# Idle products, two low halves and an early GpSimd call in a memory-attention mixer

## The chip, the cores and the metric

The kernel runs on one core of one Trainium2 chip. The metric is the device time of one execution in microseconds (us); lower is better. The engines are named as in the profile: PE (TensorE matmul), PEld (TensorE weight load), DVE (VectorE), ACT (ScalarE), POOL (GpSimd), SP (SyncE, which issues the DMAs).

## The reference, cut to what matters

Eight batches, eight heads, 576 positions, head dimension 64, 32 memory slots. First an attention over a memory, then a token and channel mixer:

```python
a = softmax(phi, axis=slots)                       # phi [8, 8, 576, 32]
k_m, v_m = einsum('bhsm,bhsd->bhmd', a, k), einsum('bhsm,bhsd->bhmd', a, v)
attn = softmax(q @ k_m.T / sqrt(64), axis=slots) @ v_m
x = attn as [8, 576, 512]
h = maximum(x.T @ w_tok1, 0) @ w_tok2              # 576 -> 256 -> 576
u = x + h.T
out = u + maximum(u @ w_ch1, 0) @ w_ch2            # 512 -> 1536 -> 512
```

The weights come as 64-bit words. The kernel turns them on the chip into a high and a low fp32r part each; a product with full precision is then three matmuls (high by high, high by low, low by high).

## The kernel before, in words

The batches are cut into 9 chunks of 512 columns for the channel mixer, and each batch into two quads of four heads (quad `(b, Q)`, tile names end in the quad). A quad runs: softmax of phi, `kvp` (or `kp` and `vp` apart in the first batch), keys turned (`Tp`, `kb`), scores `sp`, softmax `S`, the attention `aT` and its high and low parts, `Ap` and `Rp` (the token mixer), `u`. Then the chunk's channel mixer takes `uh` and `ul`: products `cp` (with `c1h`, `c1l`), their relu parts `hh` (ACT) and `hl` (DVE), products `acc` (with `c2`).

Two stages have their order set in different ways. The **front** is batches 0 and 1, the conversion of the weights and the first chunk. A planner (`plan`) with a cost and a set of buffers for every step draws up one order for all engines; the code is then written out in that order, so each engine's queue is fixed. From the second chunk on a **table of slots** (`at`, `run`) sets the order: two slots for each of a chunk's 12 products of `cp`, with steps of the next quads put at slots (`k` is the place within a slot). Instructions wait by semaphores for their inputs and for free buffers; each engine works through its queue strictly in that order.

Places that the change touches:

- **Idle products.** `ps_tile` puts `fill` matmuls of the identity by itself into a PSUM bank just before a step of the front takes that bank. They compute nothing that is read. `fill` is worked out from the planned gap of PE before the step.
- **The early GpSimd call.** Right after the constants a `partition_all_reduce` runs on a scratch tile on POOL (L104). Its result is not used. In POOL's program a library index is reloaded wherever the queue passes from plain operations (such as `TENSOR_TENSOR`) to `PARTITION_ALL_REDUCE` or back: ahead of L104, ahead of the first weight low part `w1l` (L644), and later ahead of the first `phi_max` of the slot table (L261).
- **The third batch's first quad, (2, 0)** (class `ThirdBatchQuad`, held in `second`). `a_pair` writes the high half of the attention on ACT and subtracts it on POOL for the low half (L455, L456), two pairs.
- **The next quad, (2, 1)**: `phi_max` (DVE, then POOL), `phi_exp` (subtraction on DVE, exponential on ACT), `phi_sum` (DVE, then POOL), placed at slots `m - 7`, `m - 4` and `m - 3`.

In the front two more names matter. `raww` tiles are the raw words of the token weights, turned by ACT (L610, L622, L626), DVE (L616, L633) and then split by ACT (L640) and POOL or DVE (L644). Quad (0, 1) keeps its scores in the tile `k`, whose keys are used up by `kp` before; POOL clears its tail (L1113) ahead of the exponential (L414).

Of the kernel before, what the change touches and what calls it, by code (L numbers as in the profile page):

```python
# [15 lines left out]
ALU = mybir.AluOpType  # L16
AX = mybir.AxisListType
PSUM = bass.MemoryType.PSUM
RED = bass_isa.ReduceOp

P = 128
# [7 lines left out]
def kernel(  # L29
# [25 lines left out]
    nc = tc.nc  # L55
# [36 lines left out]
    for a in range(2):  # L92
# [3 lines left out]
    small = [  # L96
        wp.tile([P, n], F32, tag=tag, name="small" + tag, bufs=bufs)
        for tag, n, bufs in (("mx", 4 * NC, 2), ("ms", 6, 1))
    ]
# [1 line left out]
        nc.gpsimd.memset(t, 0.0)  # L101
    warm = wp.tile([P, 1], F32, tag="ps", name="warm", bufs=2)
    nc.scalar.activation(out=warm, in_=small[1][:, :1], func=AF.Exp)
    nc.gpsimd.partition_all_reduce(small[0][:, :6], small[1], P, RED.max)  # L104


    w1h = wp.tile([P, NC, TT], F32R, name="w1h")
# [7 lines left out]
    def f32(t):  # L115
        return t.bitcast(F32)
# [16 lines left out]
    def wide(dtype, name):  # L133

        return sb.tile([P, NKK, CW], dtype, tag="wide", name=name, bufs=5)


    class Chunk:
        def __init__(s, c):
            s.c, s.n, s.hid = c, f"_{c}", {}  # L140
            s.uh = wide(F32R, "uh" + s.n)
            s.ul = wide(F32R, "ul" + s.n)
# [79 lines left out]
    def mixer(c):  # L222
        if c not in chunks:
            chunks[c] = Chunk(c)
        return chunks[c]
# [2 lines left out]


    class Quad:  # L230
        def __init__(s, b, Q):
            s.b, s.Q, s.n = b, Q, f"_{b}_{Q}"

# [217 lines left out]
        def a_pair(s, p):  # L451

            own, other = slice(64 * p, 64 * p + 64), slice(64 - 64 * p, P - 64 * p)
            h, l = s.pairs[p][own], s.pairs[p][other]
            nc.scalar.copy(out=h, in_=s.aT[own])  # L455
            nc.gpsimd.tensor_tensor(out=l, in0=s.aT[own], in1=f32(h), op=ALU.subtract)  # L456

        def v_pairs(s):

# [303 lines left out]
    def step(eng, us, fn, *after, take=(), use=(), move=0.0, port=False, other=None):  # L763
        steps.append(Step(eng, us, fn, after, list(take), list(use), move, port, other))
        return steps[-1]
# [630 lines left out]
    class ThirdBatchQuad(SecondQuad):  # L1396


        attend = Quad.attend

        def step_kv(s):
            s.kvp = bank([P, CW], "kvp" + s.n)
# [131 lines left out]
    for Q, h0 in ((0, 3), (1, 11)):  # L1534
        qd = quads[1, Q]
        late = 4 if not Q else 0
# [11 lines left out]
    z = second.plan_phi()  # L1548
    step("SP", 0.62, second.load_kv, take=[kv2], move=3.5)
    step("SP", 0.62, second.load_q, quads[1, 1].x_s, take=[q2], move=1.6)  # L1550
    o0, y = Room(("wide", 5)), products[-4]
    for x in range(NKK):
        y = step(
            "POOL", 1.4, lambda x=x: chunks[0].residual([x]), *a.lows, *c.lows, y,
            use=[*room0] + ([o0] if x else []), take=[] if x else [o0],
        )
# [7 lines left out]
    for z in order:  # L1564
        if z.eng == "PE":
            if z is products[0]:
                break
            gap = z.begin - max(idle, 2.0)
            if gap > 1.0 and z.take:
                z.fill = int(0.42 * gap / 0.24)  # L1570
            idle = z.end
    for z in order:
        now[0] = z
# [6 lines left out]
    def at(h, fn, *x, k=0):  # L1580
        events.setdefault((max(h, 0), k), []).append((fn, x))

    beside = {}
    for b in range(2, B):
        for Q in range(2):
            qd = second if b == 2 and not Q else Quad(b, Q)
            r = 2 * NF * b - (14 if Q else 26)
            if b == 2 and not Q:
                r = m = 2 * NF
            else:  # L1590

                m = r - (0 if b == 2 else 10 if b > 3 or Q else 8)
                at(max(m - 11, 2 * NF), qd.load_phi)
                at(m - (6 if (b, Q) == (3, 0) else 7), qd.phi_max, k=1)
                at(m - 4, qd.phi_exp, k=1)
                at(m - 3, qd.phi_sum, k=1)
                at(loaded + 1, qd.load_kv, k=1)
                at(r - 4, qd.load_q, k=1)
            loaded = m
            at(m, qd.step_kv)  # L1600
            at(m + 4, qd.values)
            if b > 2:
                at(m + 3, qd.get_keys, k=1)
            else:
                at(m + 1, qd.step_T)
            at(r + 2, qd.step_s)
            if Q or b == 2:
                at(r + 3, qd.sm2)
            else:
                beside[r + 3] = qd  # L1610
            at(r + (3 if qd is second else 4), qd.a_pair, 1)
            at(r + 6, qd.nat, k=1)
            at(r + 7, qd.v_pairs)
            at(r + 8, qd.step_A)
            at(r + 9, qd.step_R)
            for x in range(4):
                at(r + 10 + x // 2 * (1 if qd is second else 2), qd.step_u, x // 2, x % 2)
        at(2 * NF * (b - 1) + 7, lambda b=b: mixer(b).take(), k=1)
    for c in range(CHUNKS):
        h = 2 * NF * (c + 1)  # L1620
# [5 lines left out]
        if h + 1 in beside:  # L1626
            qd = beside.pop(h + 1)
# [125 lines left out]
```

## Time and profile before

| what | value |
|---|---|
| median of 3 runs | 780.65 us (780.28 to 783.66) |
| the profiled execution, its own time | 776.89 us |
| its span, first to last instruction | 775.1 us |
| mean granted TensorE clock of it | 0.993 of full speed |
| PE busy | 763.0 us, 98% of the span |
| DVE, ACT, POOL busy | 363.1, 249.6, 136.1 us |

The profile is of one execution, which took 776.89 us, of which 1.79 us lie around the span; the three timed runs took 3.4 to 6.8 us longer than it. Times inside the trace count from the start of the span. A PE that is busy is not always doing work that the result needs: idle products count as busy.

### The profile page before, as it was taken

The numbers are of one execution on the slowest core, as the hardware profiler recorded it, in microseconds if no ns is written. First come the engines' busy times: TensorE is split into PE (matmuls) and PEld (weight loads), VectorE is DVE, ScalarE is ACT, GpSimd is POOL, SyncE is SP. The second block draws the span as 40 slices with busy tenths as digits, with TensorE's granted clock in tenths as the row PEclk, the third lists the DMA queues.
The fourth block names the chain that finished last, engine by engine and source line by source line (L and its number), as shares of the span: only waits on it lengthen the run. The fifth ranks groups of instructions, "written<-read, shape, count | busy, mean of one in ns | idle before, by whom it ended". The sixth has DMA issues, their size and how long they took to land.

```text
span 775.1 us, 11131 instructions
## 1 busy us (share of the span) xinstructions
PE 763.0 (98%) x4520; PEld 633.9 (82%) x4520; DVE 363.1 (47%) x617; ACT 249.6 (32%) x481; POOL 136.1 (18%) x118
## 2 busy tenths in 40 slices
PE   7999999999999999999999999999999999999998
PEld 6777888777878888887878887888888888888887
DVE  4978874646454443635354445444352512212114
ACT  5789664232314232323223231423232311110110
POOL 1234223112211013101320121101310402002000
PEclk8999999999999999999999999999999999999999
DMA  9945420332406040514024130604040101001001
GB/s 322 417 152 206 172 99 9 89 114 84 136 3 204 1 151 2 145 60 122 30 37 169 19 134 5 203 1 150 2 120 1 32 1 54 1 1 54 1 1 54
DMA packets 52674, 68.93 MB, mean 89 GB/s; under 512 B 33680, under 2 KB 42896, under 8 KB 48400
## 3 DMA queue, kind: packets, MB, share of 16 engines
q1 hardware_dynamic: 52048, 67.71, 26.3%
q8 instruction: 35, 0.57, 0.3%
q10 hardware_dynamic: 576, 0.52, 0.2%
q14 instruction: 15, 0.12, 0.1%
HBM read 54.92 MB, written 13.30 MB: 88 GB/s over the span
## 4 chain that ended last, share of the span: by engine, by line
PE 83%; DVE 7%; issue 5%; DMA 3%; POOL 1%; ACT 1%; SPq 0%; DVEq 0%; ACTq 0%; POOLq 0%
PE cp L159 34%; PE acc L192 32%; PE u L549 7%; PE Ap L509 3%; PE u L1203 2%; DMA k<-in_kv_dram 1%; PE Rp L528 1%; DMA rawc<-in_w_ch_dram 1%; DVE o L210 1%; PE end L192 1%; PE kvp L296 1%; PE sp L392 1%; DVE S L423 1%; DVE S L399 1%; DVE mx L406 0%
## 5 line engine op out<-in xcount | busy, mean ns | idle before, releaser
L192 PE MATMUL acc<-hh,c 128*128 128x512 f32 x832 | 277.7, 394 | 0.8
L129 DVE SCALAR_TENSOR_TENSOR hl<-cp,hh 128x512 fp32r<-128x512 f32 x104 | 71.7, 689 | 271.7 <-ACT hh L126 271.7
L192 PEld LDWEIGHTS acc<-hh,c 128*128 128x128 f32 x832 | 156.2, 188 | 39.9 <-issue 6.1
L159 PE MATMUL cp<-uh,c1h 128*128 128x512 f32 x432 | 163.4, 392 | 0.0
L159 PE MATMUL cp<-ul,c1h 128*128 128x512 f32 x432 | 162.5, 390 | 0.0
L192 PE MATMUL acc<-hl,c 128*128 128x512 f32 x416 | 162.4, 390 | 0.0
L159 PE MATMUL cp<-uh,c1l 128*128 128x512 f32 x432 | 162.3, 389 | 0.0
L126 ACT ACTIVATE hh<-cp 128x512 fp32r<-128x512 f32 x104 | 61.9, 596 | 268.7 <-PE cp L159 268.7
L159 PEld LDWEIGHTS cp<-uh,c1l 128*128 128x128 f32 x432 | 81.1, 188 | 17.0
L159 PEld LDWEIGHTS cp<-ul,c1h 128*128 128x128 f32 x432 | 81.2, 188 | 16.6
L159 PEld LDWEIGHTS cp<-uh,c1h 128*128 128x128 f32 x432 | 80.6, 188 | 17.1 <-issue 1.1
L192 PEld LDWEIGHTS acc<-hl,c 128*128 128x128 f32 x416 | 78.2, 188 | 13.9
L456 POOL TENSOR_TENSOR a<-aT,a 64x576 fp32r<-64x576 f32 x24 | 34.3, 1430 | 202.2 <-ACT a L455 116.6
L204 POOL TENSOR_TENSOR o<-uh,ul 128x512 f32<-128x512 f32 x36 | 48.7, 1380 | 116.5 <-PE cp L159 46.9
L250 DVE TENSOR_REDUCE pr<-phi 128x128 f32<-128x640 f32 x22 | 29.0, 1319 | 12.5 <-ACT phi L274 8.1
L455 ACT CAST a<-aT 64x576 fp32r<-64x576 f32 x24 | 16.2, 673 | 56.0 <-DVE aT L429 55.7
L549 PE MATMUL u<-w2l,Rh 128*128 128x288 f32 x112 | 33.1, 295 | 0.0
L549 PE MATMUL u<-w2h,Rh 128*128 128x288 f32 x112 | 33.0, 295 | 0.0
L549 PE MATMUL u<-w2h,Rl 128*128 128x288 f32 x112 | 32.9, 294 | 0.0
L574 DVE TENSOR_TENSOR ul<-u,uh 128x288 fp32r<-128x288 f32 (+8 forms) x48 | 17.1, 356 | 21.8 <-ACT uh L568 21.5
L129 DVE SCALAR_TENSOR_TENSOR Rl<-Rp,Rh 128x512 fp32r<-128x512 f32 x14 | 9.6, 687 | 35.9 <-ACT Rh L126 35.9
L283 POOL PARTITION_ALL_REDUCE psr<-pr x11 | 11.9, 1081 | 70.3 <-issue 48.9
(199 smaller groups left out, 883.7 us busy)
## 6 DMA issues: line engine op xcount, KB each, us to landing
kv<-in_kv_dram SPq DMA_DIRECT2D x12, 1280.0 KB, 6.8
rawc<-in_w_ch_dram SPq DMA_DIRECT2D x12, 1024.0 KB, 7.6
q<-in_q_dram SPq DMA_DIRECT2D x16, 576.0 KB, 5.9
out_dram<-o SPq DMA_DIRECT2D x8, 1024.0 KB, 7.4
phi<-in_phi_dram SPq DMA_DIRECT2D x16, 320.0 KB, 4.0
kv<-in_kv_dram SPq DMA_DIRECT2D x6, 640.0 KB, 10.5
rows<-S SPq DMA_DIRECT2D x48, 72.0 KB, 2.0
raw<-rows SPq DMA_DIRECT2D x12, 256.0 KB, 2.8
```

Source lines behind the costliest of these rows:

```text
L126: nc.scalar.activation(out=h, in_=ps, func=AF.Relu)
L129: nc.vector.scalar_tensor_tensor(out=l, in0=ps, scalar=0.0, in1=f32(h), op0=ALU.max, op1=ALU.subtract)
L159: nc.tensor.matmul(ps, l[:, a, w], r[:, a], start=n == 0, stop=n == len(mm) - 1)
L192: nc.tensor.matmul(ps, l_[f // 2][:, f % 2, a * P : (a + 1) * P], r[:, w], start=f == start and x == 0, stop=f == end - 1 and x == 2,)
L204: nc.gpsimd.tensor_tensor(out=s.o[:, a], in0=f32(s.uh[:, a]), in1=f32(s.ul[:, a]), op=ALU.add)
L250: nc.vector.tensor_reduce(out=m.rearrange("p (i m) -> p i m", i=4), in_=s.pt.rearrange("p i j m -> p i m j"), axis=AX.X, op=op,)
L455: nc.scalar.copy(out=h, in_=s.aT[own])
L456: nc.gpsimd.tensor_tensor(out=l, in0=s.aT[own], in1=f32(h), op=ALU.subtract)
L509: nc.tensor.matmul(ps[:, :TT], a, w, start=x == 0, stop=x == len(mm) - 1)
L549: nc.tensor.matmul(ps[:, :HALF], a, r, start=x == 0, stop=x == len(mm) - 1)
L574: nc.vector.tensor_tensor(out=ch.ul[:, kk, to], in0=ps[:, :n], in1=f32(ch.uh[:, kk, to]), op=ALU.subtract)
L1203: nc.tensor.matmul(ps[:, :HALF], a, r, start=n == 0, stop=n == len(mm) - 1)
```

## The change

Three things are changed.

1. The idle products: the threshold of a planned gap falls from 1.0 to 0.3 us, the factor from 0.42 to 0.85, and a step gets three more where a DMA that it needs is planned to land late. In the written order this is 35 idle products in six places, where there were 10 in two.
2. In the third batch, quad (2, 0) has its low halves subtracted on DVE instead of POOL, and quad (2, 1) has `phi_exp` and `phi_sum` placed one slot later.
3. The early `partition_all_reduce` is left out, and with it two of POOL's library reloads; a third is no longer needed behind the low halves and stands behind the residual sums `o` instead.

```diff
-    nc.gpsimd.partition_all_reduce(small[0][:, :6], small[1], P, RED.max)
...
     class Quad:
+        low_eng = nc.gpsimd
...
             nc.scalar.copy(out=h, in_=s.aT[own])
-            nc.gpsimd.tensor_tensor(out=l, in0=s.aT[own], in1=f32(h), op=ALU.subtract)
+            s.low_eng.tensor_tensor(out=l, in0=s.aT[own], in1=f32(h), op=ALU.subtract)
...
     class ThirdBatchQuad(SecondQuad):
-        attend = Quad.attend
+        attend, low_eng = Quad.attend, nc.vector
...
             gap = z.begin - max(idle, 2.0)
-            if gap > 1.0 and z.take:
-                z.fill = int(0.42 * gap / 0.24)
+            if gap > 0.3 and z.take:
+
+                late = any(y.eng == "SP" and y.ready > z.begin - 0.5 for y in z.after)
+                z.fill = int(0.85 * gap / 0.24) + 3 * late
...
-                at(m - 4, qd.phi_exp, k=1)
-                at(m - 3, qd.phi_sum, k=1)
+                at(m - (3 if b == 2 else 4), qd.phi_exp, k=1)
+                at(m - (2 if b == 2 else 3), qd.phi_sum, k=1)
```

On PE, at the start of the program, the queue of before begins like this (`pp` are the products that turn phi, `<-ident` alone marks an idle product):

```order
L887 MATMUL pp_0_0_135<-ident 128x128 x8
L941 MATMUL pp_0_0_135<-dg_0_131,phi_0_103 128x128 x4
L941 MATMUL pp_0_0_144<-dg_0_131,phi_0_103 128x128
L941 MATMUL pp_0_1_158<-dg_1_152,phi_1_105 128x128 x4
L941 MATMUL pp_0_1_159<-dg_1_152,phi_1_105 128x128
L1043 MATMUL kp_0_176<-kv_0_109,pt_0_170 32x64 x20
L1073 MATMUL Tp_0_202<-ident,T_0_200 128x128
L1097 MATMUL sp_0_0_207<-kb_0_205,q_0_111 128x64 x8
L1097 MATMUL sp_0_0_208<-kb_0_205,q_0_111 64x64 x2
L1043 MATMUL kp_1_223<-k_1_113 32x64 x20
L887 MATMUL Tp_1_256<-ident 128x128 x2
```

And with the change, the same engine from its first product on:

```order
L888 MATMUL pp_0_0_134<-ident 128x128 x17
L942 MATMUL pp_0_0_134<-dg_0_130,phi_0_102 128x128 x4
L888 MATMUL kp_0_184<-ident 128x128 x5
L1044 MATMUL kp_0_184<-kv_0_108,pt_0_178 32x64 x20
L888 MATMUL Tp_0_215<-ident 128x128 x2
L1074 MATMUL Tp_0_215<-ident,T_0_213 128x128
L888 MATMUL sp_0_0_222<-ident 128x128 x2
L1098 MATMUL sp_0_0_222<-kb_0_220,q_0_110 128x64 x8
L888 MATMUL Tp_1_273<-ident 128x128 x5
L1074 MATMUL Tp_1_273<-ident,T_1_270 128x128
L888 MATMUL vp_0_282<-ident 128x128 x4
L1044 MATMUL vp_0_282<-kv_0_108,pt_0_178 32x64 x20
```

No product that the result needs has moved; there are 9 more idle ones ahead of the first, and groups of 5, 2, 2, 3 and 4 more between `kp`, `Tp`, `sp` and `vp`.

On POOL in the third batch, before (`o` are the first chunk's residual sums, `ISA` without names is the library reload, `prr` is the reduction that `phi_max` asks for):

```order
L204 TENSOR_TENSOR o_1241<-uh_416,ul_417 128x512 x4
L456 TENSOR_TENSOR a_2_0_1429<-aT_0_1427,a_2_0_1429 64x576
L456 TENSOR_TENSOR a_2_0_1430<-aT_0_1427,a_2_0_1430 64x576
L261 ISA
L261 ISA prr_1_1452<-pr_1_1450 128x128
L283 ISA psr_1_1533<-pr_1_1531 128x128
```

With the change, on POOL:

```order
L203 TENSOR_TENSOR o_1265<-uh_440,ul_441 128x512 x4
L262 ISA
L262 ISA prr_1_1476<-pr_1_1474 128x128
L284 ISA psr_1_1596<-pr_1_1594 128x128
L262 ISA prr_0_1600<-pr_0_1598 128x128
```

The two low halves are gone, so the reload of the library stands right behind the residual sums. DVE's queue at that place with the change:

```order
L430 STREAM_TRANSPOSE aT_0_1451<-S_0_1415 128x576
L457 TENSOR_TENSOR a_2_0_1453<-aT_0_1451,a_2_0_1453 64x576
L457 TENSOR_TENSOR a_2_0_1454<-aT_0_1451,a_2_0_1454 64x576
L251 TENSOR_REDUCE pr_1_1474<-phi_1_1364 128x128
L128 SCALAR_TENSOR_TENSOR hl_1_1480<-cp_1_1461,hh_1_1479 128x512
```

The two subtractions stand between the transpose of the attention and the reduction `pr` that feeds `prr`; before, `pr` followed the transpose at once. On ACT the exponential of quad (2, 1), `phi`, has changed places with four small copies `vv` of quad (2, 0); with the change:

```order
L121 CAST nat_0_1528<-raw_0_1448 64x128
L465 CAST vv_0_1535<-vh_0_1483 64x128 x4
L275 ACTIVATE phi_1_1364<-phi_1_1364 128x640
L121 CAST uh_1555<-rest 128x4x128
L125 ACTIVATE hh_1_1559<-cp_1_1540 128x512
L121 CAST Ah_0_1578<-Ap_0_1563 128x256
```

The copies `vv` no longer stand behind the exponential, and `Ah`, which `Rp` on PE needs, is still behind it. On DVE the sum `pr` that follows the exponential has moved from ahead of `ul`, `hl` and `Al` to behind `Al`.

## Rows read from the trace of the kernel before

**Rows 1.** The page: its first line.

```profile
span 775.1 us, 11131 instructions
```

**Rows 2.** PE's waits between 30 and 164 us, the whole list.

```profile
PE u L549 <- DVE nat L1332: 0.2, 1, 0.2
```

**Rows 3.** Busy time by stage, 12 to 22 us: PE, PEld, DVE, ACT, POOL, clock, DMA.

```profile
12.00:22.00 10.00, 9.55 (x112) 8.35 (x112) 5.71 (x13) 5.24 (x9) 0.96 (x2) 0.50 1.03 359
```

**Rows 4.** Timeline, TensorE in the front: start us, us, what, idle before.

```profile
1.56 3.49 PEld L887 LDWEIGHTS pp<-ident 128*128 128x128 f32 x16 [1.56 <-POOL mask L89]
...
6.37 2.31 PEld L941 LDWEIGHTS pp<-dg,phi 128*128 128x128 f32 x20 [1.33 <-ACT phi L923]
...
10.71 0.77 PE L1043 MATMUL kp<-kv,pt 128*32 128x64 f32 x40 [1.83 <-DMA kv<-in_kv_dram]
...
12.81 4.29 PE L1097 MATMUL sp<-kb,q 128*128 128x64 f32 x20 [0.45 <-DVE kb L1081]
...
29.53 2.69 PE L1178 MATMUL Ap<-raww,k 128*128 128x256 f32 x10 [0.20 <-DVE k L1143]
```

**Rows 5.** Timeline, ACT ahead of the first copies of pp.

```profile
8.36 1.20 ACT L610 ACTIVATE raww<-raww,mask 128x1024 f32<-128x1024 uint32 x1 [2.02 <-DMA raww<-in_w_tok_dram]
```

**Rows 6.** DMA issues between 6.1 and 6.9 us, last number us to landing.

```profile
kv<-in_kv_dram SPq DMA_DIRECT2D x1, 640.0 KB, 12.5
```

**Rows 7.** Timeline, the early GpSimd call and who stands behind it.

```profile
13.73 0.76 POOL L104 PARTITION_ALL_REDUCE smallmx<-smallms  x1 [11.08 <-issue]
...
14.27 1.10 ACT L640 CAST w1h<-raww 128x1024 fp32r<-128x1024 f32 x1 [0.66 <-DVE raww L633]
...
23.71 2.42 POOL L644 TENSOR_TENSOR w1l<-raww,w1h 128x1024 fp32r<-128x1024 f32 x1 [8.96 <-DMA rawc<-in_w_ch_dram]
...
26.41 0.74 ACT L414 ACTIVATE k<-k 128x640 f32<-128x640 f32 x1 [1.30 <-POOL k L1113]
```

**Rows 8.** Timeline, ACT and DVE in the front.

```profile
17.37 0.54 ACT L610 ACTIVATE raww<-raww,mask 128x256 f32<-128x256 uint32 x1 [2.01 <-DMA raww<-in_w_tok_tail_dram]
...
19.94 0.81 DVE L1137 TENSOR_REDUCE sm<-S 128x20 f32<-128x640 f32 x1
...
23.45 0.88 DVE L1121 TENSOR_REDUCE mx<-sp 128x16 f32<-128x512 f32 x2 [0.17 <-PE sp L1097]
...
25.05 1.69 DVE L633 SCALAR_TENSOR_TENSOR raww<-raww 128x576 f32<-128x576 f32 x1
...
32.49 0.75 DVE L633 SCALAR_TENSOR_TENSOR raww<-raww 128x576 f32<-128x576 f32 x1
```

**Rows 9.** Timeline, third batch: POOL with its reduction, and PE around Rp.

```profile
125.50 5.03 POOL L204 TENSOR_TENSOR o<-uh,ul 128x512 f32<-128x512 f32 x4 [0.77 <-POOL c L644]
...
161.34 0.72 POOL L261 PARTITION_ALL_REDUCE prr<-pr  x1 [7.00 <-issue]
...
164.49 0.39 PE L192 MATMUL acc<-hh,c 128*128 128x512 f32 x1
166.25 0.39 PE L528 MATMUL Rp<-vh,Ah 128*128 128x256 f32 x1 [1.38 <-ACT Ah L122]
...
167.84 0.40 PE L159 MATMUL cp<-uh,c1h 128*128 128x512 f32 x1
```

**Rows 10.** The chain that ended last, an undisturbed Rp: start us, us, what.

```profile
99.21 0.73 PE Rp L528 x6
```

**Rows 11.** Timeline, third batch: ACT, DVE and PE around the low halves.

```profile
150.50 1.30 DVE L250 TENSOR_REDUCE pr<-phi 128x128 f32<-128x640 f32 x1
150.61 1.37 ACT L455 CAST a<-aT 64x576 fp32r<-64x576 f32 x2 [2.94 <-DVE aT L429]
...
155.08 0.39 PE L192 MATMUL acc<-hl,c 128*128 128x512 f32 x1
```

**Rows 12.** Line L261 between 529 and 537 us: count, durations in ns, starts.

```profile
L261 POOLq MODIFY_POOL_CONFIG  x2: 6/6/6, 529.4 to 529.4; - x2
...
L261 POOL PARTITION_ALL_REDUCE prr<-pr x1: 720/720/720, 536.3 to 536.3; - x1
```

## The prediction

> **What bounds the kernel now.** I read the page first: the span is 775.1 us [rows 1], and the profiled execution took 776.89 us, 1.79 us more than it. PE is busy nearly all the time, so time can only come from PE's idle stretches, from products run at the lower clock, or from idle products that stand ahead of useful ones. Then PE's list of waits: between 30 and 164 us it holds one wait of 0.2 us [rows 2]. Whatever reaches PE earlier at 30 us is therefore kept until about 164 us, as long as the other engines keep up. Two places remain. [...] The second is one hole in the third batch: the last `acc` starts at 164.49 and the next `cp` only at 167.84 us, with `Rp` between them waiting for ACT's `Ah` [rows 9].
>
> **Front, the idle products themselves.** The eight of before (two passes each, x16 in the row) took 3.49 us, 0.436 us a product, at the lower clock; the ten real products `pp` behind them (x20), of the same shape, took 2.31 us, 0.231 us a product, so at the upper one [rows 4]. I take it that the clock rises where it did, after the first eight, at 1.56 + 3.49 = 5.05 us. The nine added ones end at 5.05 + 9 x 0.231 = 7.13 us, and the first five `pp` at 7.13 + 5 x 0.231 = 8.28 us. Nobody waits for the delay: ACT copies `pp` only behind L610, which waited 2.02 us for a DMA and ends at 8.36 + 1.20 = 9.56 us [rows 5]. The other five end at 9.44, and the five idle ones ahead of `kp` at 9.44 + 1.16 = 10.60 us, before 10.71, where `kp` starts once the DMA of `kv` has landed [rows 4]. So they cost nothing, and the DMA is the cover. If the cover is short, each costs 0.23 us. The groups ahead of `Tp` and `sp` (2 and 2, at most 0.46 us each) lie in gaps of 0.45 us or so [rows 4], cost at most 0.1 us, and I leave that out.
>
> **Front, the clock.** PE waited 1.83 us ahead of `kp`, then in short pieces up to `sp` [rows 4], and the clock fell. With those gaps filled I take it that it does not fall. Then the 4.29 us of the first `sp` become 2.15; it ends near 12.81 + 2.15 = 14.96 instead of 17.10 us. Not all of that gets through. The exponential of this quad stands on ACT behind an L610 that waits 2.01 us for a DMA and ends at 17.37 + 0.54 = 17.91 [rows 8]; 0.74 for the exponential (the same size at 26.41 [rows 7]) gives 18.65, and `sm` on DVE starts at about 18.70 instead of 19.94: -1.24 us. From `sm` to the second quad's `mx`, DVE has 23.45 - 19.94 = 3.51 us, of which 0.17 is a wait for `sp` [rows 8]; without it `mx` starts at 18.70 + 3.34 = 22.04, -1.4 us. PE must have the second `sp` by then: `vp` needs the half of `kv` issued near 6.2 that takes 12.5 us [rows 6], so 18.7, plus 0.77 as for `kp` [rows 4], plus 2.15 for `sp`: 21.6 us, in time.
>
> **Front, the early call.** POOL idles 11.08 us ahead of it; the first `w1l` then starts at 23.71, though its input from ACT was done at 14.27 + 1.10 = 15.37 us [rows 7]. With the call and both reloads gone, `w1l` runs from about 15.4 to 17.8 us. Two things follow. The clear of `k`'s tail, which held the second exponential for 1.30 us [rows 7], comes early. And DVE's L633 at 25.05 us, which took 1.69 us with `w1l` running beside it on POOL, should take the 0.75 of the same instruction at 32.49 [rows 8]: -0.94 us. On DVE `sm` of the second quad stands behind this L633, so it comes 1.4 + 0.94 = 2.35 us earlier, and so do `k` and the second `Ap`. Against this, the next `w1l` is free to start earlier too and may fall on DVE's multiplication of `k`, with the same 0.94 lost: -1.4. Bounds -2.35 and -1.4; I take **-2.0 us**, nearer to the first since the overlap must fall on just that instruction.
>
> [...]
>
> **Third batch.** The hole is what `Rp` costs beyond itself. Undisturbed, six `Rp` of 256 columns take 0.73 us, 0.12 each [rows 10], so the `acc` of 512 columns holds PE for about 0.24, an estimate: `cp` could start at 164.49 + 0.24 + 0.73 = 165.46 and starts at 167.84, so 2.4 us stand there. The chain is: `prr` at 161.34, after 7.00 us in which POOL reloads its library behind the two low halves [rows 9], then DVE's subtraction, ACT's exponential, four `vv`, `uh`, `hh` and only then `Ah`. With the change the reload stands behind the `o`, which end at 125.50 + 5.03 = 130.53 us [rows 9], and nothing of POOL's is between. Is the load paid there, or at the call? At L261 later, the configuration is written at 529.4 and the reduction starts at 536.3 us [rows 12], 6.9 us on, the same distance as the 7.00; so it runs from the configuration, and would be done by 138 us. Then `prr` follows `pr` at once, some 7 us earlier than before, and the exponential, moved half a slot later, still comes before its old time. `vv` no longer stands behind it, so `Ah` follows `Ap`. I take the whole: **-2.4 us**. If the load were still paid at the call, `prr` would come near 161 again, but `vv` has left the chain by the order alone; I bound the term below by half, -1.2.
>
> The price is on DVE: two subtractions of 64x576, about 0.75 each (the nearest row is L633 at 32.49, of the same 576 columns [rows 8]; POOL's were slower). The high halves on ACT run 150.61 to 151.98 [rows 11], so the first runs from about 151.3 to 152.05 and the second to 152.8; `pr`, 1.30 us, moves from 150.50 to 152.8 and ends at 154.1; the `hl` queued behind it, about 0.7, at 154.8. PE takes that `hl` at 155.08 [rows 11]. It fits by 0.3 us; if each step is 0.2 us longer, PE waits 0.3 us, once.
>
> **Sum.** -2.0 - 2.4 = -4.4 us: 776.89 becomes 772.5. The median of the runs shown is 3.76 us over the profiled execution; I keep that distance, so the median becomes 780.65 - 4.4 = **776.2 us**. Behind 168 us no instruction of the change lies on a wait of PE that I saw, so nothing is added there.
>
> **Rivals.** (A) the forecast.
>
> (B) The clock falls all the same in the front, since idle products fill only part of the gaps. For it: they are written from planned gaps, and DMA landings decide the true ones. Then only the early call counts: 0 to -0.94 us of the front, and -2.4: 777.3 to 778.3 us. [...]
>
> (C) The front's lead is lost again before 164 us, because a later step waits for something that did not move: a weight half converted on DVE, or the late `hl` above. For it: PE's only wait until 164 is 0.2 us, but how close the inputs come is not in that list. Against: 2 us are small next to a chunk. 780.65 - 2.4 = 778.3 us.
>
> (D) More is gained: the multiplication of `k` is free (-2.35), the gaps of PE's first 30 us shrink further, and part of what the runs have above the profile goes too: -5.5 us, 775.2 us.
>
> (E) Slower. The clock does not rise at all in the front: 17 idle products end at 1.56 + 17 x 0.436 = 8.97, ten `pp` at 13.33, five more at 15.5 us, and `kp` starts 4.8 us late. [...] It decides from where the delay at `kp`, less 0.94, is over 2.4 us. [...]
>
> (F) The change does not do what it says: the fills sit in gaps that are not on the path and the third batch's hole moves to another wait: within 0.5%, 779 to 780.5 us.
>
> **How the numbers follow.** Chances: A 0.56 (775.4 to 777.2), B 0.13, C 0.11, D 0.09, E 0.05, F 0.06. The least that a measurement of this kernel can tell from no change is about 0.5%, 3.9 us, so 776.75 us is the border of faster. D and most of A lie under it: 0.09 + 0.47 = 0.56, and I add 0.01 for the best of B. Within: 0.39. Slower than 784.6: 0.04, an E with a larger delay. Likeliest is 776.2. The range leaves E, the worst of F and the best of D out: 773.8 to 779.2 us.
>
> **What would show it right or wrong.** Clock: the granted clock from 12 to 22 us near 1.00, the first `sp` in about 2.2 us, `kp` at 10.7. Early call: `w1l` at 15.4, L633 near 23.7 in 0.75 us, the second `Ap` at 27.5. Third batch: `prr` within 1 us after `pr`, POOL's configuration near 130, no wait of PE at `Rp` over 0.3 us, `hl` on DVE done by 155 less the front's lead. Lead: `acc` of the third batch 2 us earlier. It is wrong if `kp` starts over 0.3 us late, if the clock is 0.50 there, or if a wait of PE over 0.5 us appears between 30 and 168 us that was not there.

## The result, and the profile after

The changed kernel takes 772.36 us in the median of 6 runs (770.99 to 773.15), beside 780.85 us of 6 runs of the kernel before (777.83 to 783.66): a ratio of 0.9889, 95% interval 0.9865 to 0.9913, so 8.5 us or 1.1% less. Forecast were 776.2 us and a range of 773.8 to 779.2; the time lies below the range. In a later measurement it was 771.62 against 780.67 us, ratio 0.9886 (0.9868 to 0.9903).

The profiled execution has a span of 770.0 us, 5.1 us less than the 775.1 of [rows 1]. This is the whole list of PE's waits up to 170 us. Among others, the waits of the kernel before at `kp`, `Tp`, `sp`, both `Rp` and the second `Ap` are gone.

```profile
PE pp L888 <- POOL mask L89: 1.6, 1, 1.6
PE vp L1044 <- DMA kv<-in_kv_dram: 0.6, 1, 0.6
PE u L550 <- DVE nat L1333: 0.2, 1, 0.2
```

The stage from 12 to 22 us of the same execution (columns as in [rows 3]; the third number from the end is the granted clock):

```profile
12.00:22.00 10.00, 9.43 (x149) 8.59 (x147) 7.03 (x16) 6.39 (x11) 2.61 (x2) 1.00 1.03 362
```

The clock is 1.00 where it was 0.50; the clock records of the two traces hold these two values alone. PE's timeline in the front, against [rows 4]:

```profile
1.56 5.74 PE L888 MATMUL pp<-ident 128*128 128x128 f32 x34 [1.56 <-POOL mask L89]
...
10.66 0.77 PE L1044 MATMUL kp<-kv,pt 128*32 128x64 f32 x40
...
12.63 2.38 PE L1098 MATMUL sp<-kb,q 128*128 128x64 f32 x20
...
18.58 0.77 PE L1044 MATMUL vp<-kv,pt 128*32 128x64 f32 x40 [0.56 <-DMA kv<-in_kv_dram]
...
26.78 2.69 PE L1179 MATMUL Ap<-raww,k 128*128 128x256 f32 x10
```

The first product behind the 17 idle ones started at 7.14 us (forecast 7.13), `kp` started at 10.66 (10.7), the first `sp` took 2.38 us (2.2). The idle products, x34 in the row at two passes each, change their pace at 5.1 us, from 0.43 to 0.22 us a product. The clock records of this trace begin there too, with 1.00 (those of before at 5.0 us). That the first eight ran at the lower clock, as the prediction has it, therefore rests on their times alone. The second `Ap` started at 26.78, not at the forecast 27.5. DVE and POOL in the front, to be set against [rows 7, 8]:

```profile
18.42 0.82 DVE L1138 TENSOR_REDUCE sm<-S 128x20 f32<-128x640 f32 x1 [0.97 <-ACT S L415]
19.27 0.18 DVE L1139 TENSOR_SCALAR sm<-sm 128x20 f32<-128x20 f32 x1
...
19.68 0.36 DVE L617 SCALAR_TENSOR_TENSOR raww<-raww 128x256 int32<-128x256 int32 x1
19.96 0.81 DVE L1144 TENSOR_TENSOR S<-S,sm 128x640 f32<-128x640 f32 x1
...
21.86 0.87 DVE L1122 TENSOR_REDUCE mx<-sp 128x16 f32<-128x512 f32 x2
...
23.45 0.74 DVE L634 SCALAR_TENSOR_TENSOR raww<-raww 128x576 f32<-128x576 f32 x1
...
25.81 0.82 DVE L1144 TENSOR_TENSOR k<-k,sm 128x640 f32<-128x640 f32 x1
26.55 1.30 DVE L617 SCALAR_TENSOR_TENSOR raww<-raww 128x576 int32<-128x576 int32 x1
```

```profile
16.19 2.41 POOL L645 TENSOR_TENSOR w1l<-raww,w1h 128x1024 fp32r<-128x1024 f32 x1 [13.28 <-ACT w1h L641]
18.66 0.20 POOL L1114 MEMSET k<- 64x128 f32 x1
25.96 1.27 POOL L645 TENSOR_TENSOR w1l<-raww,w1h 128x256 fp32r<-128x256 f32 x1 [7.11 <-ACT w1h L641]
```

The large `w1l` ran from 16.19 us (forecast 15.4) to 18.60 us, ahead of DVE's L617 (0.36 us) and multiplication of `S` (0.81 us), and slowed none of those shown. The clear of `k` is done long before the second exponential. The second `w1l` started 0.15 us behind the multiplication of `k`, which kept its 0.82 us, and the L617 behind it took 1.30 us, where one of the same size took 0.76 at 20.84 us with POOL idle.

Three views of the third batch stand against [rows 9]: what POOL has on line L262 between 100 and 170 us (count, ns, first and last start), POOL's timeline, and PE's.

```profile
L262 POOLq MODIFY_POOL_CONFIG  x2: 8/8/8, 127.8 to 127.8; - x2
```

```profile
151.70 0.72 POOL L262 PARTITION_ALL_REDUCE prr<-pr  x1 [23.89 <-DVE pr L251]
```

```profile
161.76 0.39 PE L191 MATMUL acc<-hh,c 128*128 128x512 f32 x1
161.99 0.28 PE L529 MATMUL Rp<-vh,Ah 128*128 128x256 f32 x1
...
162.70 0.40 PE L158 MATMUL cp<-uh,c1h 128*128 128x512 f32 x1
```

`prr` follows `pr` (150.16 to 151.48) within 0.3 us, since the reload was configured at 127.8 us, and from the last `acc` to `cp` it is 0.94 us, where it was 3.35. The price on DVE was right too: the `hl` queued behind `pr` ended at 152.08 us, 0.28 us before PE took it.

All profiles of this study can be read in one way: cut an execution at the start of the second `Ap` and at the `cp` behind the third batch's `Rp`. The span is then the sum of a front, a middle and a rest. Each row is one execution; that of e4 was the shortest of its kernel, those of e5, e6 and e10 the longest of theirs.

| kernel | second Ap starts | from it to cp | rest | span |
|---|---|---|---|---|
| before, the profile ahead of the prediction | 29.53 | 138.31 | 607.3 | 775.1 |
| changed | 26.78 | 135.92 | 607.3 | 770.0 |
| e1, before again | 31.19 | 138.53 | 608.9 | 778.6 |
| e2, idle products alone | 28.21 | 139.70 | 608.2 | 776.1 |
| e3, no early call alone | 29.92 | 137.57 | 607.3 | 774.8 |
| e4, third batch alone | 30.28 | 135.84 | 607.3 | 773.4 |
| e5, changed with the call kept | 32.10 | 135.84 | 607.3 | 775.2 |
| e6, changed with the idle products of before | 32.47 | 135.84 | 607.1 | 775.4 |
| e7, changed with the low halves on POOL | 26.99 | 135.94 | 607.2 | 770.1 |
| e8, before with the hole filled | 30.42 | 139.90 | 608.8 | 779.1 |
| e9, w1l late | 32.33 | 135.86 | 607.3 | 775.5 |
| e10, before with the later slots | 32.02 | 138.19 | 607.1 | 777.3 |
| e11, before with the low halves on DVE | 30.51 | 137.77 | 607.5 | 775.8 |
| e12, changed again | 26.26 | 135.92 | 607.3 | 769.5 |

The first two rows differ by 2.75 + 2.39 + 0 us. That is 5.1, of 8.5 measured: 3.4 us are not in this pair of profiles. The front of before stands unchanged in e1, e4, e8, e10 and e11 as well, and in each of them the second `Ap` comes later, at 30.28 to 32.02 us: the 29.53 that I predicted from is the earliest of six.

### The profile page after: what moved, and what is told of

It reads as the page before. It is cut to its first block, busy times and chain, and to the rows that moved or that the text cites. A ratio compares the mean times of both kernels' runs of the same rounds, so it can differ in the third digit from the quotient of the medians.

```text
span 770.0 us, 11222 instructions
## 1 busy us (share of the span) xinstructions
PE 763.5 (99%) x4570; PEld 635.7 (83%) x4570; DVE 361.6 (47%) x619; ACT 249.9 (32%) x481; POOL 132.5 (17%) x115
## 4 chain that ended last, share of the span: by engine, by line
PE 90%; DVE 6%; DMA 2%; issue 1%; SPq 1%; ACT 1%; DVEq 0%; ACTq 0%
PE cp L158 36%; PE acc L191 34%; PE u L550 8%; PE Ap L510 3%; DMA kv<-in_kv_dram 2%; PE u L1204 2%; PE Rp L529 1%; DVE o L209 1%; PE end L191 1%; PE kvp L297 1%; PE sp L393 1%; PE Ap L1179 1%; DVE S L424 1%; DVE S L400 1%; DVE mx L407 0%
## 5 line engine op out<-in xcount | busy, mean ns | idle before, releaser
L457 POOL TENSOR_TENSOR a<-aT,a 64x576 fp32r<-64x576 f32 x22 | 31.5, 1431 | 183.1 <-ACT a L456 116.7
L262 POOL PARTITION_ALL_REDUCE prr<-pr x11 | 7.9, 720 | 101.9 <-issue 42.5
```

The source lines that it names most:

```text
L457: s.low_eng.tensor_tensor(out=l, in0=s.aT[own], in1=f32(h), op=ALU.subtract)
```

## The experiments

**e1, before again.** No edit: the profile ahead of the prediction is one execution, and the question was what the others have that it lacks.

> The kernel before, unchanged, to see what lies between its profiled execution (776.89) and its timed runs (about 780.8). Theory V (variable clock in the front): the executions differ among themselves; spans run from 775 to 782 us, and the longer the span the lower the mean granted clock: 4 us lost at half speed are 8 us of span at the lower level, 0.005 less of mean clock, so about 0.988 where the profile had 0.993. A profiled execution of 779 or more shows the lower clock for longer in the first 30 us, and its second Ap later than 29.5 by as much. Rival O (the distance lies elsewhere): mean clock 0.993 in all executions, second Ap within 0.5 us of 29.5, and the extra time in the third batch's hole, later, or around the span.

780.17 us median (778.43 to 784.93, 12 runs). With the runs of the kernel before that were made beside it there are 47 spans, from 773.9 to 783.1 us, and only two lie under the 775.1 of the profile that I predicted from: it was among the shortest executions. The mean clocks fall, loosely, from 0.995 at the short end to 0.987 at the long one, as theory V has it. But the new profile, whose span of 778.6 us is close to the median of these (778.5), has its extra 3.5 us in two places, and neither is the first clock rise that I had in mind: from 12 to 22 us its clock is 0.66, above the 0.50 of the first profile. First, POOL, DVE and PE in the front:

```profile
21.39 2.68 POOL L644 TENSOR_TENSOR w1l<-raww,w1h 128x1024 fp32r<-128x1024 f32 x1 [7.19 <-PE vp L1043]
```

```profile
21.72 3.03 DVE L1143 TENSOR_TENSOR S<-S,sm 128x640 f32<-128x640 f32 x1
...
27.27 0.74 DVE L633 SCALAR_TENSOR_TENSOR raww<-raww 128x576 f32<-128x576 f32 x1
...
29.63 1.41 DVE L1143 TENSOR_TENSOR k<-k,sm 128x640 f32<-128x640 f32 x1
```

```profile
24.90 0.63 PE L1152 MATMUL at<-ident,S 128*128 128x128 f32 x4 [1.94 <-DVE S L1143]
...
31.19 2.69 PE L1178 MATMUL Ap<-raww,k 128*128 128x256 f32 x10 [0.84 <-DVE k L1143]
```

`w1l`, which stands behind the reload after the early call, started at 21.39 us here and not at 23.71, so it fell on the multiplication of `S` and not on L633: 3.03 us for an instruction that takes 0.81 in the changed kernel (19.96 us), while L633 had its 0.74. `w1l` began 0.33 us before it and ended at 24.07; the multiplication ended 0.68 us behind that, so it reads as one that waited for `w1l` and then took most of its own time; what the two engines share is not shown. The multiplication of `k` took 1.41 us instead of 0.82 as the next `w1l` ran from 29.62 to 30.36, and ended 0.68 us behind it as well: the collision that the prediction feared after the change happened here, in the kernel before. The second `Ap` is 1.66 us later than in the first profile of before.

All profiles together bear this out. Eight are of kernels with the early call; in seven of these the large `w1l` slowed one DVE instruction, by 0.94 (the first profile), 2.22 (e1), 1.76 (e2), 0.71 (e4), 2.22 (e5), 2.21 (e10) and 2.23 us (e11), and in e8 none: 1.5 us on average. Of five without the call (the changed kernel, e3, e6, e7, e12) none lost anything to the large `w1l`. But it isn't all that lengthens a front. In e4, e8 and e10 PE waited 1.90, 1.40 and 1.65 us at `vp` for the DMA of `kv`, and the clock from 22 to 30 us was 0.62, 0.68 and 0.50, where the first profile has 1.00.

Second, the stages behind the third batch's hole, in which PE waited 1.49 and 0.51 us at `Rp`:

```profile
168.13 0.39 PE L528 MATMUL Rp<-vh,Ah 128*128 128x256 f32 x1 [1.49 <-ACT Ah L122]
...
169.15 0.39 PE L528 MATMUL Rp<-vh,Al 128*128 128x256 f32 x1 [0.51 <-DVE Al L123]
```

```profile
168.00:172.00 4.00, 3.36 (x13) 2.65 (x14) 2.99 (x5) 0.68 (x2) 0.87 (x2) 0.77 0.00 0
172.00:176.00 4.00, 4.00 (x22) 3.57 (x21) 0.96 (x2) 1.00 (x2) 0.00 (x0) 0.81 0.02 4
```

The clock fell behind the wait and came back; 0.23 and 0.19 of 4 us are 1.7 us, which is the 1.6 that the rest has over 607.3. In the first profile both of these stages read 1.00. So what the timed runs have over that profile is no fixed distance: in this execution it sits in the two places that the change mends.

**e2, the idle products alone.**

```diff
-            if gap > 1.0 and z.take:
-                z.fill = int(0.42 * gap / 0.24)
+            if gap > 0.3 and z.take:
+                late = any(y.eng == "SP" and y.ready > z.begin - 0.5 for y in z.after)
+                z.fill = int(0.85 * gap / 0.24) + 3 * late
```

> Before, with the idle products of the change alone (35 in six places). Theory V: they carry the unexplained part; mean clock 0.999 or more in every execution, spread of the runs under 2.5 us, median 780.8 - 3.9 - 1.4 = about 775.5. Rival O: only the front's clock loss of the profiled execution goes, -1.4: about 779.4, with the spread of before.

779.54 us (777.5 to 783.23, 12 runs) beside 780.3 of before, ratio 0.9995 (0.9972 to 1.0018): nothing that can be told from no change, and the spread stays. The variable clock in the front alone is not the explanation. The profile has the clock at 1.00 up to 30 us and the second `Ap` at 28.21; but L633 took 2.51 us beside `w1l`, the reload behind the low halves took 8.04 us, and the clock fell at the hole:

```profile
22.92 2.51 DVE L633 SCALAR_TENSOR_TENSOR raww<-raww 128x576 f32<-128x576 f32 x1
```

```profile
164.00:168.00 4.00, 1.61 (x7) 1.41 (x8) 3.50 (x5) 1.86 (x5) 1.08 (x1) 0.82 0.00 0
168.00:172.00 4.00, 4.00 (x16) 3.23 (x16) 0.71 (x2) 0.70 (x2) 0.70 (x1) 0.75 0.00 0
```

In this profile the lead of the front is spent: the middle is 1.4 us and the rest 0.9 us longer than in the first profile of before.

**e3, no early call alone.**

```diff
-    nc.gpsimd.partition_all_reduce(small[0][:, :6], small[1], P, RED.max)
```

> Before without the early partition_all_reduce (its result is not used) alone. [...] Rival O in one form, that the call with its two reloads is what varies from run to run: about 777, spread under 2.5 us.

776.33 us (772.77 to 779.85, 12 runs), ratio 0.9943 (0.9921 to 0.9966): 4.0 us, half of the whole gain, from a line that I had priced at 0.94. The profile differs from that of e1 in both places. `w1l` ran at 16.67 us and slowed no DVE instruction on the chain. And the third batch's hole was small, as the reload behind the low halves took 5.92 us:

```profile
160.97 0.72 POOL L260 PARTITION_ALL_REDUCE prr<-pr  x1 [5.92 <-issue]
```

```profile
165.88 0.39 PE L527 MATMUL Rp<-vh,Ah 128*128 128x256 f32 x1 [0.29 <-ACT Ah L121]
```

Against e1 it has 1.27 us less in the front, 0.96 in the middle and 1.6 in the rest. Against the first profile of before its second `Ap` is 0.39 us later, as PE waited 1.25 us at `vp` for `kv` and the clock fell, to 0.71 from 22 to 30 us: measured against that execution, the gain would not be seen in the front at all.

**e4, the third batch's part alone.**

```diff
-        attend = Quad.attend
+        attend, low_eng = Quad.attend, nc.vector
...
-                at(m - 4, qd.phi_exp, k=1)
-                at(m - 3, qd.phi_sum, k=1)
+                at(m - (3 if b == 2 else 4), qd.phi_exp, k=1)
+                at(m - (2 if b == 2 else 3), qd.phi_sum, k=1)
```

> Before with the third batch's part alone (low halves on VectorE, exponential and sum half a slot later). Theory V: the hole of 2.4 us closes and nothing else: about 778.4, spread as before. Rival O in another form, that this hole is wider in the timed runs than in the profile: about 774.5, spread under 2.5 us.

776.88 us (775.18 to 778.56, 12 runs), ratio 0.9958 (0.9939 to 0.9977): 3.4 us, more than the 2.4 of the hole, and a spread of 3.4 instead of 6.5 us. It lies between the two expectations. In its profile PE does not wait at `Rp`, and the rest is 607.3. The three parts alone gain 0.8 + 4.0 + 3.4 = 8.2 us, near the 8.5 of the whole. That is partly luck, as the parts do not simply add: the 0.8 can't be told from nothing, and e5 below, which has the idle products and the third batch's part, gains 6.3 us, where 0.8 + 3.4 is 4.2.

**e5, the changed kernel with the early call kept.**

```diff
+    nc.gpsimd.partition_all_reduce(small[0][:, :6], small[1], P, RED.max)
```

> The changed kernel with the early partition_all_reduce kept (idle products and third batch as changed). Theory P: the call costs through its library reload, which ends at another time in each execution (the first w1l started at 23.7, 21.4, 22.4 and 22.4 us in the profiles so far), so that w1l on GpSimd falls on this or that DVE instruction with two SBUF inputs (3.03 us for 0.81, 2.51, 1.69 and 1.46 for 0.75): about 2 us on DVE's chain, so 774.5, spread over 3 us, and the second Ap at 28 us or later. Rival Q: the 4 us that the kernel without the call gained came from the third batch's hole (0.8 us in its profile, 1.9 to 2.9 in the others); the hole being closed here, 772.4 to 773, spread about 2 us.

774.03 us (773.4 to 777.0, 11 runs) beside 780.29, ratio 0.9942 (0.9923 to 0.9961). Theory P has the time (774.5), the spread and a late second `Ap` (32.10). So the call costs 1.7 us by the medians even where the hole is closed; that the rest of the 4.0 of e3 came from the third batch, as the rival said, is an inference, since the idle products differ too. Its profile, the longest of its executions, has `w1l` at 23.66 beside an L635 of 256 columns that took 2.64 us (0.42 in the changed kernel, at 21.52 us), but also a `kv` that landed late:

```profile
23.92 2.64 DVE L635 SCALAR_TENSOR_TENSOR raww<-raww 128x256 f32<-128x256 f32 x1
```

```profile
20.99 0.77 PE L1045 MATMUL vp<-kv,pt 128*32 128x64 f32 x40 [1.97 <-DMA kv<-in_kv_dram]
```

Behind that wait the clock fell here as well, to 0.57 from 22 to 30 us, with all idle products in place. Whether the reload also delays such DMAs is not shown: this `kv` took 12.4 to 14.1 us from issue to landing in the eight profiles with the call and 11.9 to 13.2 in the six without.

**e6, the changed kernel with the idle products of before.**

```diff
-            if gap > 0.3 and z.take:
-                late = any(y.eng == "SP" and y.ready > z.begin - 0.5 for y in z.after)
-                z.fill = int(0.85 * gap / 0.24) + 3 * late
+            if gap > 1.0 and z.take:
+                z.fill = int(0.42 * gap / 0.24)
```

> The changed kernel with the ten idle products of before (no early call, third batch as changed). If the parts add: 772.4 + 0.8 = 773.2, clock 0.993 to 0.995 in most executions. Rival: with the call gone the front is set by PE and its clock, and the idle products carry their full worth: 774.4 or more.

773.67 us (770.73 to 777.2, 8 runs), ratio 0.9927 (0.9902 to 0.9951), nearer to the sum of the parts than to the rival. That is 1.3 us over the changed kernel, with overlapping intervals; the spans go from 768.9 to 775.4 us and the clocks from 0.989 to 1.000, where the changed kernel has 0.999 or more in every execution. What the idle products buy, as far as eight runs can tell, is chiefly that the executions are alike: the best without them is as short as with them.

**e7, the changed kernel with the low halves on GpSimd.**

```diff
-        attend, low_eng = Quad.attend, nc.vector
+        attend = Quad.attend
```

> The changed kernel with the two low halves back on GpSimd (the exponential and the sum stay half a slot later). If the reload behind the low halves makes the hole: it is back, 2 us or more of PE's waits at Rp, and the median is 772.4 + 2.4 to 3.4 = 774.8 to 775.8 with a spread of 4 us. Rival: the later exponential alone takes vv and pr off the chain, and nothing is lost: 772.4, no wait of PE at Rp over 0.3 us.

772.81 us (771.42 to 774.78, 6 runs), ratio 0.9918 (0.9893 to 0.9944): by the median the rival holds. In the profile `prr` came after a reload of 5.68 us, the shortest of all, and PE did not wait at `Rp`.

```profile
157.52 0.72 POOL L260 PARTITION_ALL_REDUCE prr<-pr  x1 [5.68 <-issue]
```

But this is one of the three short executions (771.42 to 771.87 us). The other three took 773.75 to 774.78, more than any of the changed kernel (773.15 at most), with a mean clock of 1.000, and none of them was profiled. So that the low halves may stay on POOL at no cost is shown for the short executions only.

**e8, before with idle products in the hole.**

```diff
             ps = bank([P, NT, 256], "Rp" + s.n)
+            for _ in range(7 if s is second else 0):
+                nc.tensor.matmul(ps[:, 0, :P], ident, ident, start=True, stop=True)
```

> Before, with seven more idle products in PE's queue right ahead of Rp in the third batch (1.6 us of work in a wait of 1.9 us or more; the wait itself stays). Theory H: in most executions the clock falls after this wait, and that is what the single profile of before did not show: median 780.3 - 1.5 = 778.8, the lowest mean clocks gone (none under 0.989). Rival: the clock there costs nothing: 780.3; should the products stand in the way, up to 0.3 more.

779.74 us (776.92 to 780.88, 12 runs) beside 780.29, ratio 0.9994 (0.9975 to 1.0014). As the theory has it, the longest executions are gone (780.9 at most, 784.3 in the runs of before) and no mean clock is under 0.993, where before goes down to 0.987; the median moved by 0.55 and not by 1.5, which is nearer to the rival. In the profiled execution the reload took 8.44 us, so that PE still waited behind the seven products,

```profile
168.76 0.39 PE L530 MATMUL Rp<-vh,Ah 128*128 128x256 f32 x1 [1.24 <-ACT Ah L122]
...
169.75 0.39 PE L530 MATMUL Rp<-vh,Al 128*128 128x256 f32 x1 [0.48 <-DVE Al L123]
```

and the clock still fell, to 0.80 from 168 to 172 us and 0.77 from 172 to 176: the rest is 608.8 us. The experiment supports the loss behind the hole but doesn't size it.

**e9, the changed kernel with w1l made late.**

```diff
             part = s.parts[x]
+            for _ in range(18 if part.name == "w1_0" and eng is nc.gpsimd else 0):
+                nc.gpsimd.memset(f32(part.l), 0.0)
             eng.tensor_tensor(
```

> The changed kernel with 18 clears of w1l (128x1024 each) on GpSimd ahead of the first subtraction w1l: no library reload, only a GpSimd that is busy, so that w1l starts near 20 us instead of 16.2. [...]

776.48 us (771.98 to 779.05, 9 runs) beside 780.67, ratio 0.9941 (0.9915 to 0.9967), and 771.62 for the changed kernel on the same chip: 4.9 us lost with no reload. A GpSimd that is merely busy is thus enough to lose time; theory P of e5, about 2 us on DVE's chain, holds in kind and was too mild. Its profile is of one of the longer executions (777.26 us); POOL, DVE, PE and two stages:

```profile
21.16 2.41 POOL L647 TENSOR_TENSOR w1l<-raww,w1h 128x1024 fp32r<-128x1024 f32 x1
```

```profile
20.20 0.91 DVE L1141 TENSOR_SCALAR sm<-sm 128x20 f32<-128x20 f32 x1
...
21.34 2.52 DVE L617 SCALAR_TENSOR_TENSOR raww<-raww 128x256 int32<-128x256 int32 x1
```

```profile
24.74 1.09 PE L1155 MATMUL at<-ident,S 128*128 128x128 f32 x4 [2.13 <-ACT raww L623]
```

```profile
12.00:22.00 10.00, 9.16 (x153) 8.41 (x144) 6.57 (x14) 6.00 (x8) 9.40 (x10) 1.00 1.03 361
22.00:30.00 8.00, 5.87 (x21) 4.03 (x20) 7.90 (x14) 4.11 (x8) 1.77 (x2) 0.59 1.01 413
```

An instruction of 0.36 us (19.68 us in the changed kernel) took 2.52, the multiplication of `S` behind it came late, PE waited 2.13 us, and then the clock fell too, to 0.59 from 22 to 30 us, all idle products notwithstanding: the collision is paid twice. Not all of the loss is `w1l`'s, though. The clears themselves, the last of which ended at 21.08 us, held up a `TENSOR_SCALAR` of DVE on the same chain, 0.91 us for 0.18, and the tail of the token weights, behind which ACT's first exponential stands, landed 0.93 us later than in the changed kernel's profile. Of the 5.55 us by which the second `Ap` is late, then, about 0.93 are this DMA's, 0.73 the clears', 2.16 `w1l`'s and most of what remains the lower clock's. Two of its nine executions have spans of 770.2 and 770.3 us, as short as the changed kernel.

**e10 and e11, the two halves of the third batch's part, each alone on the kernel before.** The diffs are the two hunks of e4: the slots in e10, `low_eng` in e11.

> Before, with the exponential and the sum of the third batch half a slot later alone (low halves on GpSimd, early call and ten idle products as before). Theory H: prr still waits for the reload behind the low halves, but the four vv (1.2 us on ACT) no longer stand between the exponential and Ah; the hole shrinks by 1.2 us and the clock behind it falls less often: 780.3 - 1.2 - 0.8 = 778.3. Rival: the order alone closes it, 776.9 as with both parts; or, with prr at 161 or later, nothing is won: 780.3.

> Before, with the third batch's low halves on DVE alone (exponential and sum where they were). Theory H: the reload is done long before pr, prr follows it at once, and the hole closes whole, with the clock's loss behind it: 776.9, no wait of PE at Rp over 0.3 us. Rival: without the later slot the exponential waits on ACT for prr and holds up the copies nat and hh behind it, which leaves a wait of 1 us or more: 778 or more.

777.09 us (775.29 to 779.1, 6 runs; ratio 0.9951, 0.9932 to 0.9969) and 777.34 us (776.24 to 778.01, 6 runs; 0.9958, 0.9942 to 0.9974). Either alone has the whole gain of e4 in time. For the slots the rival was right by the time and not by its mechanism: in the profile, with a reload of 7.50 us, PE still waited 0.64 and 0.40 us at `Rp`, so the hole was not closed, but the clock behind it was 1.00 and the rest 607.1 us. For the low halves theory H was right: PE did not wait at the third batch's `Rp`. The middle of e11 is long all the same (137.77 us), mostly because its second `Ap`, at the lower clock (0.62 from 30 to 34 us), took 4.26 us instead of 2.69, which belongs to the front.

**e12, the changed kernel again.** No edit.

> The changed kernel once more, beside the other three on one chip: 772.4, spread about 2 us, mean clock 0.999 or more in every execution, second Ap between 26.5 and 27.1 us, the first w1l within 0.3 us of 16.2, no wait of PE at Rp.

771.62 us (770.87 to 772.32, 5 runs), spans 769.1 to 770.5 us, clock 1.000 in all; second `Ap` at 26.26, 0.24 us earlier than the window I gave, `w1l` at 15.95. Against e1, a middling execution of before, it has 4.93 us less in the front, 2.61 in the middle and 1.6 in the rest, together 9.1.

## Why the prediction was wrong

The direction and the mechanisms were right, and the account between the two profiles was near (-4.4 us forecast, -5.1 measured); the time was not. The step that failed is in the sum: "The median of the runs shown is 3.76 us over the profiled execution; I keep that distance". The distance was no overhead. After the change it is 0.6 us (772.36 against 771.78, the profiled execution's own time). In e1 it lies in the front (1.66 us, `w1l` on other DVE instructions) and behind the hole (1.6 us, the clock), both of which the change takes away. That it lies there in most executions is borne out by the later fronts of e4, e8, e10 and e11, by the clock that fell at the hole in e2 and e8 too, and by e3 and e4, which each gained more than the first profile had to give; how it divides between collisions, late DMAs and the clock is not shown. The hint stood in the table: the profiled execution was shorter than all three timed runs, so its waits were likely to be mild ones.

Term by term:

- **Idle products:** right. They cost nothing, with the starts behind them forecast to 0.1 us, and the clock held at 1.00. Alone they gain nothing measurable (e2); in the one profile of e2 a collision and the hole took the lead back.
- **Early call:** right in mechanism, mis-sized. The 0.94 us of L633 is what the collision cost in one execution; in five of the other seven profiles with the call it cost 1.8 to 2.2 us on one DVE instruction, as the late `w1l` of e9 did, and in e1 and e9 1.94 and 2.13 us of waiting on PE at once. The bound should have been the length of `w1l`, 2.4 us, since what it falls on differs: L633 in before, e2 and e4, the same conversion of 256 columns in e5, the multiplication of `S` in e1, an L617 in e9. Of the 4.0 us (e3) 1.7 remain when the hole is closed (e5).
- **Front as a whole:** -2.0 forecast, -2.75 between the profiles, -4.4 from e1 to the changed kernel. The feared delay at the multiplication of `k` did not come; it stood in the kernel before, in e1 and e11 (1.41 and 1.37 us for 0.82).
- **Third batch:** -2.4 forecast and -2.39 between the profiles; 3.4 us in the runs (e4). That the clock can fall behind the hole (0.77 in e1, 0.75 in e2 and 0.80 in e8 from 168 to 172 us, 1.00 in the first profile) explains it in kind; e8 does not size it. The bound for the order alone, -1.2, was right in kind: with it (e10) the waits fell to 1.04 us, from 1.89. In the median either half alone gained as much as both (e10, e11), though half of the executions of e7 were longer than those of the changed kernel.
- **Rivals:** B, C, E and F did not happen. D, more gained, was the right side, but at 775.2 us it was still 2.8 us too long, as it changed single terms and took only a part of the distance to the runs.

Open is why the reload behind the low halves was shorter without the early call (5.92 and 5.68 us in two profiles, 7.00 to 8.44 in five with it), how often the clock falls behind the hole, and whether the reload costs anything by itself, which no run here takes apart from `w1l`'s lateness; a handful of profiles can't say.

## What to carry to other kernels

Ask of the one profile where it stands among the runs before making the sum against it: where it is shorter than they are, its waits are likely to understate what removing them gains. A long GpSimd instruction whose start varies, as that of `w1l` did behind the reload (21.39 us in e1, 23.71 in the first profile), is to be priced at its own length, 2.4 us here, against whatever it may meet on DVE's chain; here that was L617, L633 or the multiplication of `S`. A PE wait that it opens, 2.13 us in e9, is to be priced with the lower clock behind it, 0.59 from 22 to 30 us there. A useless call can be the dearest line of a front.

## What the runs showed of the hardware

- In the profile of before two `MODIFY_POOL_CONFIG` records of POOL stand at each of the 32 passages between plain operations and `PARTITION_ALL_REDUCE`; one pair more stands at 1.1 us. The reload from the end of the low halves to `prr` took 7.00, 7.14, 8.04, 8.44, 7.50, 5.92 and 5.68 us in seven profiles. Where it was configured early, at 127.8 us for a reduction at 151.70, nothing of it was left to wait for: `prr` began 0.22 us behind `pr`.
- One DVE instruction of 0.36 us took 2.52 (e9), one of 0.81 took 3.03 (e1), beside a GpSimd subtraction of 2.4 to 2.7 us. A DVE `TENSOR_SCALAR` of 0.18 us took 0.91 beside GpSimd clears (e9).
- PE's clock fell about waits of 1.2 to 2.4 us in some executions (e1, e2 and e8 at the hole, 0.77, 0.75 and 0.80 from 168 to 172 us; e9 in the front, to 0.59 from 22 to 30 us), also behind 1.25 to 1.97 us at `vp` (e3, e4, e5, e8, e10: 0.71, 0.62, 0.57, 0.68 and 0.50 from 22 to 30 us), and did not in others (the first profile of before, 1.38 and 0.51 us at `Rp`); behind the hole it cost up to 1.7 us.
